# RWKV-6 attention with a GELU MLP behind it: each product, evacuation, sum, bank fill and block copy becomes a step of its own, in a new order

## The chip, the cores and the metric

One core of one Trainium2 chip runs the whole kernel. The metric is device time in microseconds, the median of several executions. Engines in the text: PE is TensorE, PEld its weight load, DVE is VectorE, ACT is ScalarE, POOL is GpSimd, SP is SyncE, which here issues most DMAs. Each engine works through its own list of instructions in the order in which the program wrote them, and waits on semaphores where an instruction needs another engine's result.

## The reference

The first half is a recurrence over 768 positions for 4 x 8 heads of width 48, the second an MLP on the 3072 tokens with 384 channels:

```python
for t in range(S):
    cur = einsum('bhd,bhe->bhde', u * k[t], v[t])
    y[t] = einsum('bhd,bhde->bhe', r[t], state + cur)
    state = w[t][..., None] * state + einsum('bhd,bhe->bhde', k[t], v[t])
x = y.transpose(0, 2, 1, 3).reshape(3072, 384)
h = x @ w_in                       # 384 -> 2048
out = (0.5 * h * (1 + erf(h / sqrt(2)))) @ w_out
```

All of it is float32.

## The kernel before

**Tiles and stages.** The 3072 tokens are eight tiles of 384 (half of one batch each). `attention(x, unit)` and `mlp(x)` are generators: each `yield` ends a step. The loop at the end of the kernel runs stage x: the attention of tile x beside the MLP of tile x-1, and the first steps of the attention of tile x+1. A string `PLAN[x]` says which generator makes its next step: "." the MLP of tile x-1 (in stage 0 the first half of the heads, unit 0), "s" what is left of the attention of tile x (in stage 0 unit 1), "f" the attention of tile x+1, "l" the loads on SP, "c" the conversion of the weights from 64-bit words, "w" sums of weights, "x" the five sums of the finished x, `sums_of_x`. The order in which steps are made is the order in every engine's list, so PLAN alone decides what queues behind what. After the loop the MLP of tile 7 runs alone.

**The attention of a tile from 2 on** (`quarters`). DVE makes sums of products of k and r for blocks of four positions (L427 to L470; the next tile's part starts with four multiplies, L441) and small totals of w (L462). `plain` (ACT, three copies, L610) and `lay_out` (DVE, two multiplies, L615, L616) lay out r. Then come three bursts of small matmuls (L641) for blocks of 4 and three for blocks of 16, each into a pair of PSUM banks, of which there are two pairs; `copy_quarters` empties a pair, for 4 with three masked copies on DVE (L674), for 16 with six copies on ACT (L657). k is transposed in four blocks on DVE (L589), and twelve blocks are moved by DMAs from SP (L584), four by ACT (L751). From these come the kv products (L768), the state chain on DVE (`chain_states`, L784, L789), the inside products (L810), a small "fence" copy on DVE (L822), the products with the state (L857), and the copies of y into xT (ACT L880, L883; six DMAs L887).

**The MLP of a tile from 1 on.** Both matrix products use fast schemes with fewer multiplications. Up (`h_halves`): for each of four groups q seven products, with the letters of the new code: A x00, E with t1, B completes the bank of A, F, G and D accumulate in a bank `u`, which is filled with a copy of A's result, and C completes the bank of E. ACT evacuates each: gelu, a copy into g, or a save that an accumulating DMA from POOL (L1029), for q = 3 an add on DVE (L1031), adds to g. A step is a product with its evacuation and what hangs on it. Down (`g_fast`): twenty products a to t of sums of g (`G_SUMS`, DVE, L1185) in the fixed order of `G_ORDER`; six chains of products share four banks (`G_BANKS`), two of which are filled with zeros first (L1162); results go to rows by ACT (L1173) or are added on DVE (L1175). A step here is the sums that a product needs, the product (L1190), its result, and the fill of the next bank. The last group's last products, D3 with its gelu and two more, are run behind product a. The two banks `mm` hold A and E in turn, then the chains of a and of b.

**Tile 0** uses plain products (`h_plain`, L1115, `g_plain`, L1126), in stage 1.

Of the kernel before, what the change touches and what calls it, by code (L numbers as in the profile page):

```python
# [10 lines left out]
F32 = mybir.dt.float32  # L11
# [29 lines left out]
        ".lls.....slscs.lsslll.sl.sls..sl.lscsl..sss.lscs.lscs.ss.clll.s..s.cccss...wss..ss.ff"  # L41
    ),
    1: (
        "c.scscc.cs.c.cs.ccscccs.w.lcscccss.ccccc.lwcs.scc..cc.c.ccsc.cc.lcccc.ccsc.cl.cc.sclccclws"
        ".scs..s.cscllcc.wcs.ccwlw.wcsccs.fww.s.f.f...f..wwfwfx.wf..fx.fxlfxffxw"
    ),
    2: (
        "www....wlwsw.ww..w..wws.....sss.wws.sws..ss.slss..ws.wss.w.s.sslssww.ws.s...lss..l.lss.lsl"
        "s.l..s.f...sf.f.f.x.xx.f.lxx"
    ),  # L50
    3: (
        "ss.l...ss.sl.s.s.....s...ss.ss.ssll.s..lsss.s.s.sss..sssssss.s...l.s....sl.sll...s.s.fsff."
        ".fs.fl...xxx.ffxfxf"
    ),
    4: (
        "ll........ss.....s.s...ssl..s.sl.sss...s.ssss...sss.s.s.l.ssssl.ss..s....ss.lss.l.slfs.f.f"
        ".f.xl.xxfxfffxff"
    ),
# [4 lines left out]
    6: (  # L63
        "s..s...s.s....ls.ss..s...ssls...ss..sss.ss.ss.....sss.s.s..sss.ls.....sss.ll.lslss.lslf..s"
        "f.fffs.lx.x.xffffxx"
    ),
    7: (
        ".......ss....s.s...s.ssssss...sss.ss...sss..ssss.s....s.s..s..s..s.s.s.s.ss..x.x...xxx"
# [26 lines left out]
W_ORDER = "empsiclratkdjfnbohqg"  # L95

# [6 lines left out]
def kernel(  # L103
# [298 lines left out]
    def attention(x, unit):  # L402
# [190 lines left out]
        def quarters():  # L593
# [13 lines left out]
            def plain(h):  # L607
                m, r4, t4, s0, s1, s2 = views(h)
                for z, f in ((s0[:, :, :, 0:h], 1), (s1[:, :, :, 0:h], 2), (s2, 3)):
                    nc.scalar.copy(out=z, in_=r4[:, :, :, f, :])  # L610

            def lay_out(h):
                m, r4, t4, s0, s1, s2 = views(h)
                z = s1[:, :, :, h:]
                nc.vector.tensor_mul(z, r4[:, :, :, 3, :], t4[:, :, :, 2:3].to_broadcast(z.shape))  # L615
                nc.vector.tensor_mul(s0[:, :, :, h:], s1, t4[:, :, :, 1:2].to_broadcast(s1.shape))  # L616

            plain(FINE)
            lay_out(FINE)
            yield  # L620
            n_b = np_ * NI
            for h in QUARTERS:
# [27 lines left out]
                def copy_rows(first, behind, d, g):  # L650

                    for p in range(2):
                        for a, rows in ((1, slice(0, 2 * h)), (0, slice(0, h)), (2, slice(2 * h, 3 * h))):
# [3 lines left out]
                            nc.scalar.copy(out=at[z, g, first:behind, (a + 1) * h:], in_=d[z, :, :, to] if g == slice(None) else d[z, :, to])  # L657

                def copy_quarters(first, behind, d):
                    if isinstance(d, list):  # L660
                        for g in range(2):
                            copy_rows(first, behind, d[g][:, 0:(behind - first) * 3 * C // 2].rearrange("p (n x) -> p n x", n=behind - first), g)
                        return
                    d = d[:, :, 0:(behind - first) * 3 * C // 2].rearrange("p g (n x) -> p g n x", n=behind - first)
                    if m == 1:
                        copy_rows(first, behind, d, slice(None))
                        return
                    an = at[:, :, first:behind].rearrange("p g n (m x) -> p g n m x", m=m)
                    o = 0
                    for a in range(3):  # L670
# [3 lines left out]
                        nc.vector.copy_predicated(out=an[:, :, :, :, (a + 1) * h:], mask=mask.to_broadcast(data.shape), data=data)  # L674
                        o += w_q
# [13 lines left out]
                copy_quarters(*parts_of[0], ds[0])  # L689
                yield  # L690
# [7 lines left out]
                if not last:  # L698
                    plain(4 * h)
# [9 lines left out]
                if not last:  # L709
                    lay_out(4 * h)  # L710
# [6 lines left out]
                for z, d in list(zip(parts_of, ds))[1:]:  # L717
                    copy_quarters(*z, d)
                    yield
# [253 lines left out]
    def sums_of_x(x):  # L973

        assert x in done and (x == 1 or (x - 1, "h") in behind)
# [7 lines left out]
    def mlp(x):  # L983


        xT = xT_of.pop(x)
        gs = {}

        def store(row0, o_sb, c0=0):
            nc.sync.dma_start(out=out[row0:row0 + 128, c0:c0 + o_sb.shape[1]], in_=o_sb)  # L990
# [4 lines left out]
        late = []  # L995

        def h_halves():

            x00, t1, x10, x11, l0, l1 = (xT[:, c, b * HT:(b + 1) * HT] for c in range(3) for b in range(2))
            t2, t3, t4, l01 = x_sums  # L1000

# [6 lines left out]
            def two(o, q, *factors, start=False):  # L1008
                for i in range(2):
# [12 lines left out]
            def saved(o):  # L1022
                z = wk.tile([128, DM], F32, name="o_sb", bufs=2)
                nc.scalar.copy(out=z, in_=o)  # L1024
                return of_two(z)

            def add_to(q, o, z):
# [5 lines left out]
            def first(q):  # L1033
                a_of[q] = h_bank()
                two(a_of[q], q, (w(0, 0), x00), start=True)
# [3 lines left out]
            def second(q):  # L1039
                two(a_of[q], q, (w(0, 1), x10), (w(0, 2), l0))  # L1040
                gelu(q, 0, 0, of_two(a_of[q]))

            def third(q):
                two(z_of[q], q, (s(4), x11), (w(0, 2), l1))
                add_to(q, g_of(q, 0, 1), saved(z_of[q]))

            def fourth(q):
                two(u_of[q], q, (w(1, 1), t4), (w(1, 2), l01))
                gelu(q, 1, 0, of_two(u_of[q]))

            def fifth(q):
                z_of[q] = h_bank()
                two(z_of[q], q, (s(1), t1), start=True)
                nc.scalar.copy(out=g_of(q, 1, 1), in_=of_two(z_of[q]))

            def sixth(q):
                two(u_of[q], q, (s(2), t2))
                nc.scalar.copy(out=g_of(q, 0, 1), in_=of_two(u_of[q]))

            def seventh(q):  # L1060
                two(u_of[q], q, (s(3), t3), (w(1, 2), l1))
                add_to(q, g_of(q, 1, 1), saved(u_of[q]))

            def h_bank():
                return bank("h_ps")[:, 0:2 * HT]

            a_of, z_of, u_of = {}, {}, {}
            for group in (0, 2, 1, 3):
                gs[group] = gp.tile([128, FG, T], F32, name="g")
            for q in range(HK):  # L1070
                assert q // 2 in ready
                first(q)
                if q > 1:
                    gelu(q - 2, 1, 1, g_of(q - 2, 1, 1))
                yield
                if q:
                    third(q - 1)
                    yield
                    seventh(q - 1)
                    yield  # L1080
                else:
                    fifth(q)
                    yield
                second(q)
                yield
                if q:
                    fifth(q)
                    yield
                sixth(q)
                yield  # L1090
                if q:
                    fourth(q - 1)
                    gelu(q - 1, 0, 1, g_of(q - 1, 0, 1))
                    yield
            q = HK - 1
            seventh(q)
# [225 lines left out]
```

## Time and profile before

| | us |
|---|---|
| median of 3 runs | 595.72 |
| the runs | 592.74, 596.96, 595.72 |
| the profiled execution | 595.25 |
| its span, first to last instruction | 593.4 |
| last stage, MLP of tile 7 alone | 59.0 |
| copies out of burst pairs on ACT, L657, 108 of them | 39.0 |
| state chain on DVE, L784, 160 of them | 29.3 |

A row of the profile names engine, line, operation, tile written and tiles read, shape, and count; "busy" is the time in which at least one instruction of the group ran, and the idle time in brackets is what the engine waited just before, with the instruction that ended the wait. The granted TensorE clock was 1.00 in every stage.

### The profile page before, as it was taken

What the parts mean: (1) busy time and instruction counts of PE and PEld (TensorE: products, weight loads), DVE (VectorE), ACT (ScalarE), POOL (GpSimd) and SP (SyncE); (2) the same over time, 40 slices, a digit from 0 to 9 for tenths busy, and PEclk for the clock granted to TensorE, in tenths of its full rate; (3) what the DMA queues carried; (4) which work ended last, traced back from release to release, by engine and by line L of the source; (5) the groups of instructions that cost most, each with busy time, mean ns of one, the idle gap of its engine ahead of it and who ended that gap; (6) DMA issues with size and microseconds to landing.
All of it is one profiled execution on the core that took longest, in us unless ns stands there. A gap on an engine that the chain in (4) does not pass through costs nothing.

```text
span 593.4 us, 17546 instructions
## 1 busy us (share of the span) xinstructions
PE 569.0 (96%) x7530; PEld 509.6 (86%) x7544; DVE 451.5 (76%) x880; ACT 290.1 (49%) x634; POOL 58.7 (10%) x63
## 2 busy tenths in 40 slices
PE   6789999999999999999999999999999999999997
PEld 3566656679899998999998989999999899999997
DVE  6878947999988987896786987897796987640171
ACT  2366989235642558035562356425544465525520
POOL 3100000002100130003100121003100021002200
PEclk9999999999999999999999999999999999999999
DMA  6668661134250642245213632425315342203401
GB/s 236 197 196 304 229 216 56 39 107 55 36 140 14 182 67 37 78 141 94 28 32 87 166 83 28 94 46 125 40 19 149 92 55 31 40 12 66 54 1 40
DMA packets 61854, 55.07 MB, mean 93 GB/s; under 512 B 32337, under 2 KB 46929, under 8 KB 61777
## 3 DMA queue, kind: packets, MB, share of 16 engines
q1 hardware_dynamic: 50256, 45.62, 25.6%
q0 software_dynamic: 11424, 8.26, 10.8%
q8 instruction: 59, 0.97, 0.7%
q14 instruction: 19, 0.15, 0.1%
q10 hardware_dynamic: 96, 0.07, 0.1%
HBM read 36.24 MB, written 4.72 MB: 69 GB/s over the span
## 4 chain that ended last, share of the span: by engine, by line
PE 84%; DVE 7%; ACT 4%; DMA 2%; issue 2%; SPq 1%; DVEq 0%
PE h_ps L993 17%; PE u_ps L1190 15%; PE u_ps L993 15%; PE o_ps L1190 11%; PE o_ps L1126 5%; PE h_ps L1115 5%; PE d L641 4%; PE d L504 3%; PE kv_ps L768 2%; PE y_ps L857 2%; PE y_ps L810 2%; DMA rkw<-in_rkw_dram 2%; ACT g L1020 2%; ACT a_sb L657 1%; DVE rkw L470 1%
## 5 line engine op out<-in xcount | busy, mean ns | idle before, releaser
L993 PE MATMUL h_ps<-xT,w_in_sb 128*128 128x192 f32 x560 | 111.7, 330 | 2.0 <-DVE xT L980 1.6
L1029 POOL DMA_DIRECT2D g<-o_sb x42 | 50.7, 1244 | 488.4 <-ACT o_sb L1024 486.6
L993 PEld LDWEIGHTS h_ps<-xT,w_in_sb 128*128 128x128 f32 x560 | 93.1, 190 | 6.2 <-DVE xT L980 2.2
L1190 PE MATMUL u_ps<-w_out_sb,g 128*128 128x192 f32 x224 | 41.5, 329 | 0.0
L993 PE MATMUL u_ps<-s,w_in_sb 128*128 128x192 f32 x224 | 41.2, 327 | 0.0
L657 ACT COPY a_sb<-d 32x320 f32<-32x320 f32 (+5 forms) x108 | 39.0, 361 | 3.4 <-PE d L641 1.6
L1190 PE MATMUL o_ps<-t,g 128*128 128x192 f32 x224 | 40.0, 327 | 0.6 <-ACT o_sb L1024 0.6
L1190 PEld LDWEIGHTS o_ps<-t,g 128*128 128x128 f32 x224 | 36.9, 190 | 0.9 <-ACT o_sb L1024 0.9
L993 PEld LDWEIGHTS u_ps<-s,w_in_sb 128*128 128x128 f32 x224 | 37.1, 190 | 0.2
L1190 PEld LDWEIGHTS u_ps<-w_out_sb,g 128*128 128x128 f32 x224 | 36.9, 190 | 0.3
L1173 ACT ACTIVATE o_sb<-u_ps 128x192 f32<-128x192 f32 x21 | 6.9, 330 | 53.9 <-PE u_ps L1190 53.7
L1126 PE MATMUL o_ps<-w_out_sb,g 128*128 128x384 f32 x96 | 33.0, 494 | 0.0
L1190 PE MATMUL u_ps<-w_extra,g 128*128 128x192 f32 x168 | 31.6, 331 | 1.5 <-ACT u_ps L1162 1.5
L641 PE MATMUL d<-kx,rkw 64*64 64x96 f32 x1152 | 30.0, 247 | 2.5 <-ACT a_sb L657 1.7
L1115 PE MATMUL h_ps<-xT,w_in_sb 128*128 128x384 f32 x96 | 32.3, 492 | 0.0
L641 PEld LDWEIGHTS d<-kx,rkw 64*64 64x64 f32 x1152 | 25.1, 133 | 7.5 <-ACT a_sb L657 3.3
L1190 PEld LDWEIGHTS u_ps<-w_extra,g 128*128 128x128 f32 x168 | 27.4, 190 | 3.3 <-ACT u_ps L1162 3.0
L674 DVE COPY_PREDICATED a_sb<-quarter,d 128x480 f32<-128x480 uint8 (+5 forms) x54 | 23.1, 438 | 9.1 <-PE d L641 7.9
L1031 DVE TENSOR_TENSOR g<-g,o_sb 128x384 f32<-128x384 f32 x14 | 7.7, 548 | 29.2 <-ACT o_sb L1024 29.1
L784 DVE SCALAR_TENSOR_TENSOR st<-st,tot_sb,kv_ps 128x48 f32<-128x48 f32 x160 | 29.3, 256 | 0.7 <-PE kv_ps L768 0.6
L504 PEld LDWEIGHTS d<-rkw 64*64 64x64 f32 x1152 | 19.1, 134 | 12.5 <-issue 7.0
L1020 ACT ACTIVATE g<-g 128x384 f32<-128x384 f32 x56 | 28.4, 520 | 1.1 <-DMA g<-o_sb 0.8
(163 smaller groups left out, 1195.6 us busy)
## 6 DMA issues: line engine op xcount, KB each, us to landing
rkw<-in_rkw_dram SPq DMA_DIRECT2D x54, 256.0 KB, 3.7
g<-o_sb POOLq DMA_DIRECT2D x42, 192.0 KB, 3.6
raw<-in_w_out_dram SPq DMA_DIRECT2D x8, 768.0 KB, 4.5
v_in<-in_v_dram SPq DMA_DIRECT2D x8, 584.0 KB, 4.6
raw<-in_w_in_dram SPq DMA_DIRECT2D x5, 768.0 KB, 6.8
rkw<-kx SPq DMA_DIRECT2D x72, 48.0 KB, 2.0
out_dram<-o_sb SPq DMA_DIRECT2D x17, 192.0 KB, 2.0
rkw<-in_rkw_dram SPq DMA_DIRECT2D x6, 384.0 KB, 5.2
```

Of the source, the lines that this page charges most:

```text
L504: nc.tensor.matmul(d[half[p], g, n * width:(n + 1) * width], lhsT=kc[half[g], b, i, p], rhs=right(half[g], b, i, p), start=True, stop=True)
L641: nc.tensor.matmul(o[half[p], i * 3 * C // 2:(i + 1) * 3 * C // 2], lhsT=kc[half[g], n // NI, n % NI, p], rhs=rx[half[g], 2 * n + p], star ...
L657: nc.scalar.copy(out=at[z, g, first:behind, (a + 1) * h:], in_=d[z, :, :, to] if g == slice(None) else d[z, :, to])
L674: nc.vector.copy_predicated(out=an[:, :, :, :, (a + 1) * h:], mask=mask.to_broadcast(data.shape), data=data)
L768: nc.tensor.matmul(kv_ps[half[g], p, i * D:(i + 1) * D], lhsT=k_t(b, i, p, g), rhs=vs(b, i, g)[half[p], 0:D], start=True, stop=True)
L784: nc.vector.scalar_tensor_tensor(out=stq[:, q, c], in0=stq[:, q, c - 1] if c else b4[:, q, NC - 1], scalar=totq[:, q, c:c + 1], in1=kvs[q ...
L993: nc.tensor.matmul(o, lhsT=lhsT, rhs=rhs, start=start, stop=True, skip_group_check=True)
L1020: nc.scalar.activation(out=g_of(q, a, b), in_=z, func=AF.Gelu)
L1029: nc.gpsimd.dma_start(out=o, in_=z, accum_op=ALU.add)
L1115: nc.tensor.matmul(h_ps, lhsT=w_in_sb[:, f // FI, j, f % FI * 128:(f % FI + 1) * 128], rhs=xT[:, j, :], start=(j == 0), stop=(j == NJ - 1))
L1126: nc.tensor.matmul(o, lhsT=gs[f // FG][:, f % FG, i * 128:(i + 1) * 128], rhs=w_out_sb[:, f, :], start=(f == 0), stop=(f == NF - 1))
L1190: nc.tensor.matmul(held[chain], lhsT=a(G_PRODUCTS[z])[:, j], rhs=w_place[z][:, j], skip_group_check=True, start=G_BANKS[chain][0] == "m" a ...
```

## The change

`PLAN` is replaced for all stages; a "." is now a single operation, so strings are longer. In the MLP of tiles 1 to 7 `h_halves`, `g_fast` and `G_ORDER` give way to two tables of operations and `ORDER[x]`, a list of 131 operations for each tile: the letters with a group number are those above (capitals products, small letters what follows them), "+" a sum, "=" a product, "!" its result to the rows, "<" the fill of a bank. `ORDER[7]` lists the operations in the order in which the code before makes them. In the attention each copy of a burst's pair, each copy of `plain`, each half of `lay_out` and each block copy of k on ACT gets its own `yield` (76 steps for a tile where there were 43). The rows of the output get their buffer when first written instead of at the start of the second product. No operation is added, removed or resized. Tables 2, 3, 5 and 6 and most of PLAN are left out of the diff below; this table counts from all of them how many large products (A to G, a to t) stand between two places of a stage, before and after the change:

| stage | ahead of the first burst | first to last burst of 16 | k transposes to kv | kv to inside | inside to state products | state products to the end | C3 to product b |
|---|---|---|---|---|---|---|---|
| 2 | 9, 5 | 3, 3 | 9, 14 | 4, 4 | 4, 3 | 6, 7 | 2, 4 |
| 3 | 15, 14 | 2, 2 | 10, 11 | 6, 3 | 2, 1 | 5, 6 | 2, 3 |
| 4 | 17, 18 | 1, 2 | 7, 10 | 3, 3 | 0, 0 | 5, 5 | 2, 4 |
| 5 | 15, 19 | 2, 2 | 8, 11 | 4, 2 | 1, 0 | 5, 5 | 2, 3 |
| 6 | 16, 18 | 1, 2 | 8, 10 | 3, 3 | 1, 1 | 3, 4 | 2, 4 |
| 7 | 15, 15 | 2, 2 | 12, 10 | 4, 3 | 0, 1 | 6, 6 | 2, 2 |

```diff
 PLAN = {
     0: (
-        ".lls.....slscs.lsslll.sl.sls..sl.lscsl..sss.lscs.lscs.ss.clll.s..s.cccss...wss..ss.ff"
+        "lllll.lll.lll.l.s.s.ssssss..sc.sssl.s.lcl.s.s.s.s..lcls.ssc.s.c.s.s.cs..cscss.s.sfwf."
     ),
...
     5: (
-        "l........ss....s.l..ss.sssl.s.l.ss.lsss...ssssl..sss.s...s.ss.s..s....ss.s.slll.f.sf.sff.f"
-        "x...xl.xxx"
+        "s..s.s.......s..s..s....s.......s..s........sss..s...sss....sl.ss.sss.sssss....s...ss.sss...s....s.."
+        "s.ls..sl.s.ss.s.s.s.s.s...s..s..s.s.s.sls.s.ssllsss.s.....sss.s..........s..s.........ss..s.llss..l."
+        ".ss.f...f.f..fxx.xxl.fx."
     ),
...
-G_ORDER = (
-    "a +22 +e5 b +e2 i +03 g +23 +e0 +e1 k +e3 +01 +E3 +E2 j +00 h +20 c +e4 m +E0 "
-    "+E4 q l n s p f o t r d e"
-)
 W_ORDER = "empsiclratkdjfnbohqg"
+ORDER = {
+    1: (
+        "A0 a0 E0 e0 F0 B0 C0 b0 f0 A1 G0 c0 a1 E1 g0 B1 e1 F1 k0 f1 D0 b1 G1 A2 l0 C1 g1 d0 a2 j0 B2 c1 l1 E2 F2 "
+        "e2 b2 i0 k1 A3 f2 j1 C2 D1 c2 d1 G2 a3 g2 E3 F3 D2 e3 d2 l2 f3 i1 B3 b3 C3 k2 G3 <i c3 g3 k3 l3 =a i2 i3 "
+        "D3 j2 +01 d3 <g j3 =i +00 !b =b +23 =g +03 !a =k +22 +e0 +e5 +e1 !g +e2 +e3 =j +E2 !j +E3 !k =h !h =c =m "
+        "!c +20 !m +e4 =q !q =l <p =n !n !i +E0 +E4 !l =s !s =o =p !p =f =t !f !o =r !t !r =d =e !e !d"
+    ),
...
+    4: (
+        "A0 E0 a0 e0 B0 F0 b0 C0 f0 A1 G0 c0 k0 a1 F1 g0 E1 B1 f1 D0 b1 e1 d0 G1 A2 C1 l0 a2 g1 B2 c1 F2 b2 E2 i0 "
+        "A3 e2 k1 D1 d1 C2 a3 l1 j1 f2 j0 G2 c2 k2 g2 F3 E3 e3 i1 f3 B3 D2 C3 c3 l2 d2 i2 G3 j2 +22 g3 b3 =a k3 "
+        "D3 l3 +e5 <i i3 +e2 d3 !a j3 +03 +23 =b +01 <g =g +e0 =k +e1 =i =j !g +e3 =c !k !j =h +E3 !d +E2 !h +00 "
+        "+20 =m !i =q !m !q +e4 =l +E4 !l =n +E0 =s !c !s <p !n =p =f !p !f =o =t !o !b !t =r !r =d =e !e"
+    ),
...
+    7: (
+        "A0 a0 E0 e0 B0 b0 F0 f0 A1 a1 C0 c0 k0 G0 g0 l0 B1 b1 E1 e1 F1 f1 D0 d0 i0 A2 a2 j0 C1 c1 k1 G1 g1 l1 B2 "
+        "b2 E2 e2 F2 f2 D1 d1 i1 A3 a3 j1 C2 c2 k2 G2 g2 l2 B3 b3 E3 e3 F3 f3 D2 d2 i2 G3 g3 l3 j2 C3 c3 k3 =a !a "
+        "D3 d3 i3 j3 +22 +e5 =b !b <i +e2 =i !i <g +03 =g !g +23 +e0 +e1 =k !k +e3 +01 +E3 +E2 =j !j +00 =h !h "
+        "+20 =c !c +e4 =m !m +E0 +E4 =q !q =l !l =n !n =s !s <p =p !p =f !f =o !o =t !t =r !r =d !d =e !e"
+    ),
+}
...
                     nc.scalar.copy(out=z, in_=r4[:, :, :, f, :])
+                    yield
 
             def lay_out(h):
                 m, r4, t4, s0, s1, s2 = views(h)
                 z = s1[:, :, :, h:]
                 nc.vector.tensor_mul(z, r4[:, :, :, 3, :], t4[:, :, :, 2:3].to_broadcast(z.shape))
+                yield
                 nc.vector.tensor_mul(s0[:, :, :, h:], s1, t4[:, :, :, 1:2].to_broadcast(s1.shape))
 
-            plain(FINE)
-            lay_out(FINE)
+            yield from plain(FINE)
+            yield from lay_out(FINE)
...
                             nc.scalar.copy(out=at[z, g, first:behind, (a + 1) * h:], in_=d[z, :, :, to] if g == slice(None) else d[z, :, to])
+                            yield
...
                 assert (x - 1, "at") in behind
-                copy_quarters(*parts_of[0], ds[0])
-                yield
+                yield from copy_quarters(*parts_of[0], ds[0])
...
                 nc.scalar.copy(out=block_of_kt(z, z), in_=kb[z * 32:(z + 1) * 32, z])
+                yield
...
+            def begin(of, q, o, *factors):
+                of[q] = o[:, 0:2 * HT]
+                two(of[q], q, *factors, start=True)
+
+            def fill(q):
                 u_of[q] = bank_u(q)[:, 0:2 * HT]
                 nc.scalar.copy(out=u_of[q], in_=a_of[q])
 
+            return {
+                "A": lambda q: begin(a_of, q, bank("h_ps"), (w(0, 0), x00)),
+                "a": fill,
+                "B": lambda q: two(a_of[q], q, (w(0, 1), x10), (w(0, 2), l0)),
+                "b": lambda q: gelu(q, 0, 0, of_two(a_of[q])),
+                "C": lambda q: two(z_of[q], q, (s(4), x11), (w(0, 2), l1)),
+                "c": lambda q: save(q, 0, z_of[q]),
+                "k": lambda q: add(q, 0, 1),
+                "D": lambda q: two(u_of[q], q, (w(1, 1), t4), (w(1, 2), l01)),
+                "d": lambda q: gelu(q, 1, 0, of_two(u_of[q])),
+                "E": lambda q: begin(z_of, q, bank("h_ps"), (s(1), t1)),
+                "e": lambda q: nc.scalar.copy(out=g_of(q, 1, 1), in_=of_two(z_of[q])),
+                "F": lambda q: two(u_of[q], q, (s(2), t2)),
+                "f": lambda q: nc.scalar.copy(out=g_of(q, 0, 1), in_=of_two(u_of[q])),
+                "G": lambda q: two(u_of[q], q, (s(3), t3), (w(1, 2), l1)),
+                "g": lambda q: save(q, 1, u_of[q]),
+                "l": lambda q: add(q, 1, 1),
+                "i": lambda q: gelu(q, 0, 1, g_of(q, 0, 1)),
+                "j": lambda q: gelu(q, 1, 1, g_of(q, 1, 1)),
+            }
...
+            def product(p):
+                chain = chain_of[p]
+                if chain not in held:
+                    assert G_BANKS[chain][0] == "m"
+                    open_bank(p)
+                for j in range(FG):
+                    multiply(held[chain], a(G_PRODUCTS[p])[:, j], w_place[p][:, j], G_BANKS[chain][0] == "m" and p == chain[0] and j == 0)
...
-            for z in tokens:
-                if z[0] == "+":
-                    x_, op, y_ = G_SUMS[z[1:]].split()
-                    (nc.vector.tensor_add if op == "+" else nc.vector.tensor_sub)(*(a(i) for i in (z[1:] if z != "+E0" else "20", x_, y_)))
-                    continue
...
-        row0 = x * T
-        if x:
-            yield from h_halves()
-            yield from g_fast()
-        else:
+            return {"+": add, "<": open_bank, "=": product, "!": end}
+
+        if not x:
             yield from h_plain()
             yield from g_plain()
+            return
+        ops = {**h_ops(), **g_ops()}
+        order = ORDER[x].split()
+        assert len(set(order)) == len(order) == 18 * HK + len(G_SUMS) + 2 * len(G_PRODUCTS) + sum(z[0] == "u" for z in G_BANKS.values())
+        for z in order:
+            ops[z[0]](int(z[1:]) if z[1:].isdigit() and z[0] not in "+<=!" else z[1:])
+            behind.add((x, z))
+            yield
```

More of the change, by code (lines that the diff above doesn't have):

```diff
@@ L1060, in seventh @@
[L1060 to L1080, printed above, removed]
-                else:
[L1082 to L1094, printed above, removed]
@@ L1169, in end @@
                     i, n = int(z[2]), int(z[3])
+                    if i not in rows:
+                        rows[i] = wk.tile([128, DM], F32, name="o_sb", bufs=2)
                     to = rows[i][:, n * HM:(n + 1) * HM]
```

155 lines of the change are left out of this document (60 added, 95 removed), and 20 rows, old and new, of the table ORDER.

## The prediction

> **What bounds the kernel now.** I read the page from the top, then the busy time of each stage, then who waits on TensorE, then the places in order of time. Stage x is the attention of tile x beside the MLP of tile x-1; the cuts are the starts of each tile's first product A0.
>
> ```profile
> span 593.4 us, 17546 instructions
> PE 569.0 (96%) x7530; PEld 509.6 (86%) x7544; DVE 451.5 (76%) x880; ACT 290.1 (49%) x634; POOL 58.7 (10%) x63
> ```
>
> Second view, the stages. Columns: stretch, its length, busy us of PE, weight load, DVE, ACT, POOL, granted clock, DMA share, GB/s.
>
> ```profile
> 0.00:45.00 45.00, 33.22 (x1082) 23.65 (x1096) 34.42 (x106) 19.70 (x33) 7.98 (x21) 1.00 0.65 209
> 45.00:125.60 80.60, 80.59 (x1073) 50.78 (x1074) 64.83 (x106) 53.92 (x77) 0.00 (x0) 1.00 0.46 155
> 125.60:194.00 68.40, 66.90 (x833) 63.25 (x834) 63.32 (x121) 33.10 (x81) 7.37 (x6) 1.00 0.37 82
> 194.00:261.70 67.70, 66.79 (x851) 63.49 (x850) 56.86 (x106) 32.75 (x80) 7.23 (x6) 1.00 0.37 79
> 261.70:329.60 67.90, 66.29 (x832) 63.48 (x832) 53.17 (x101) 32.78 (x80) 7.23 (x6) 1.00 0.35 80
> 329.60:398.20 68.60, 66.76 (x851) 63.63 (x850) 59.12 (x111) 32.74 (x80) 7.23 (x6) 1.00 0.36 81
> 398.20:467.80 69.60, 67.22 (x838) 63.83 (x836) 56.38 (x108) 33.47 (x81) 7.20 (x6) 1.00 0.37 81
> 467.80:534.40 66.60, 66.05 (x846) 63.27 (x847) 46.95 (x93) 32.37 (x79) 7.28 (x6) 1.00 0.27 48
> ```
>
> TensorE bounds it from 45 us on. Stage 1 idles 0.01 us. In stages 2 to 7 length minus busy PE gives 1.50, 0.91, 1.61, 1.84, 2.38 and 0.55: 8.8 us. No other engine fills a stage; DVE comes nearest (63.32 of 68.40). The operations stay, so a new order can win little beyond those 8.8 us and what stage 0 holds.
>
> Third view: who ended TensorE's waits in stages 2 to 7 (us in total, times, longest).
>
> ```profile
> PE d L641 <- ACT a_sb L657: 1.7, 3, 0.6
> PE h_ps L993 <- DVE xT L980: 1.6, 2, 1.0
> PE u_ps L1190 <- ACT u_ps L1162: 1.2, 4, 0.3
> PE o_ps L1190 <- ACT o_sb L1024: 1.1, 2, 0.6
> PE d L641 <- DVE kx L616: 0.8, 1, 0.8
> PE y_ps L857 <- DVE fence L822: 0.8, 3, 0.4
> PE kv_ps L768 <- DMA rkw<-kx: 0.4, 1, 0.4
> PE y_ps L810 <- DVE st L784: 0.4, 1, 0.4
> PE h_ps L993 <- DMA xT<-ysb: 0.4, 1, 0.4
> ```
>
> Eighteen waits, 8.4 us. A wait costs a little more than its row says:
>
> ```profile
> 306.09 1.46 PE L1190 MATMUL u_ps<-w_extra,g 128*128 128x192 f32 x8
> 307.39 1.46 PE L1190 MATMUL o_ps<-w_out_sb,e 128*128 128x192 f32 x8
> ```
>
> One product lasts 1.46 us, yet the next starts 1.30 after it. Idle time counts from the modelled end, so a stall loses its row plus 0.16. That makes 1.30 the price of an eight-matmul step (B, C, D, G, "="), and 0.65 that of A, E and F.
>
> **The change part by part.** It adds and removes no operation; counts of matmuls, evacuations and DMAs are the same, and so are the runs of small matmuls between large ones (41 in the tables of stages 2 to 7 before, 40 after). Only waits change.
>
> *Waits that the coarse steps made.* Three places:
>
> ```profile
> 296.36 2.58 ACT L657 COPY a_sb<-d 32x320 f32<-32x320 f32 x6
> 298.99 0.56 PE L641 MATMUL d<-kx,rkw 64*64 64x96 f32 x16 [0.57 <-ACT a_sb L657]
> 230.98 1.57 PE L1190 MATMUL o_ps<-w_out_sb,g 128*128 128x192 f32 x8 [0.57 <-ACT o_sb L1024]
> 232.76 1.57 PE L1190 MATMUL u_ps<-w_extra,g 128*128 128x192 f32 x8 [0.21 <-ACT u_ps L1162]
> ```
>
> The last burst of the 16-step needs the bank pair that six copies (2.58 us) empty. In stages 2, 4 and 6, where the wait is, 2.6, 1.3 and 1.3 us of large products stood between the first burst and the last; the new tables put 3.25, 2.6 and 2.6 there. Product b takes the bank of C3 two products later, while its evacuation c3 queues on ACT; the new tables for stages 2 to 6 leave three or four. The fill "<i" was issued behind d3, i3 and j3; now it stands ahead of d3 in stages 2 to 6 (stage 7 keeps it behind, but i is the sixth product there instead of the third). So 1.7 + 1.2 + 1.1 = 4.0 us and nine restarts of 0.16: -5.4. If an evacuation ahead of the fill is late, as much as the old rows comes back, no more than 0.73 a place.
>
> *First burst and kv.* The wait on kx (0.8, stage 5) goes: 18.2 us of products now precede that burst in its stage, 14.95 before: -1.0. kv waits on the block moves:
>
> ```profile
> 310.93 0.62 SPq L584
> 311.60 2.03 DMA rkw<-kx
> 313.76 1.57 PE L768 MATMUL kv_ps<-v_in,rkw 64*64 64x48 f32 x90 [0.40 <-DMA rkw<-kx]
> ```
>
> In stage 4 seven products lay between transposes and kv, now ten: 3.9 us more against 0.4: -0.6. Elsewhere 10 to 14 lie there (8 to 12 before). On SP at most one load (stage 3) stands among the twelve moves, 0.6 us by the move's row, within that cover. Stage 2 moves the first burst from nine products into the stage to five; nearest row is the 0.8 wait of the same burst: 0 to 0.8, I take +0.6: six of DVE's weight-sum steps still stand ahead of it (eleven before).
>
> *Into the end of a tile.* From kv to the inside products:
>
> ```profile
> 452.30 1.57 PE L1190 MATMUL u_ps<-w_out_sb,g 128*128 128x192 f32 x8
> 456.40 1.63 PE L810 MATMUL y_ps<-a_sb,v_in 64*64 64x64 f32 x96
> 452.58 2.18 DVE L784 SCALAR_TENSOR_TENSOR st<-st,tot_sb,kv_ps 128x48 f32<-128x48 f32 x12
> 454.94 1.48 DVE L784 SCALAR_TENSOR_TENSOR st<-st,tot_sb,kv_ps 128x48 f32<-128x48 f32 x8
> 456.34 3.06 DVE L441 SCALAR_TENSOR_TENSOR kx<-rkw,u_sb 128x384 f32<-128x384 f32 x4
> 459.97 1.45 PE L857 MATMUL y_ps<-rkw,st 64*64 64x64 f32 x80 [0.45 <-DVE fence L822]
> ```
>
> The y pairs reuse kv's banks, so the state chain must end first: kv ends at 452.3, the chain at 456.4, 4.1 us; three products (3.9) just cover it. Before, the six stages had 4, 6, 3, 4, 3, 4 products there; now 4, 3, 3, 2, 3, 3. Stage 5 has 2.6 us against 3.9 to 4.1: +1.4. Stages 3 and 7 lose their cover while row adds still stand inside the chain: +0.45 each. The fence waits (0.8) stay: stage 7 loses one, stage 5 gets one, and stage 6 still puts the next tile's four multiplies (3.06) on DVE ahead of the fence. Behind these DVE instructions wait the sums of x and so A0's successors: in stage 4 one block of small totals leaves the queue ahead of the sums and the 0.57 at the start of stage 5 goes: -0.7. In stage 6 four products follow the last y matmuls instead of three, which covers the xT DMA (0.4); the sums still come late: -0.4.
>
> Stages 2 to 7: -5.4 -1.0 -0.6 +0.6 +1.4 +0.9 -0.7 -0.4 = **-5.2 us**. The last MLP runs table 7, which is today's order step for step: 0.
>
> *Stages 0 and 1.* Stage 1 stays full of TensorE. In stage 0, twelve of the seventeen load steps now come before the first unit's update of r (two of them before). DVE has 34.42 us of work in 45 and cannot start until data lands, so I take 0, between -2 and +3. What may be lost:
>
> ```profile
> PEld d L504 <- issue: 6.5, 7, 1.4
> PE d L504 <- issue: 2.5, 3, 1.3
> ```
>
> These are waits of the matmul queue in the first 46 us that no semaphore explains, at a DMA share of 0.65; none of over a microsecond appears after. The Trainium skill, Runtime: NRT & Kernel Launch, "Instruction fetch mechanics", says that instruction fetch is hidden by the sequencer's own pace; by it fuller queues would cost nothing. The trace does not fit that well, but names no cause.
>
> The profiled execution took 595.25 us, 1.85 outside its span, and the median of the runs shown is 595.72. 595.25 - 5.2 = **590.0 us**.
>
> **The rivals.** *Slower: blocked queues* (0.24). The block copies and burst copies, six to twelve in a row before, now stand singly between evacuations that each wait for a product in an in-order queue.
>
> ```profile
> ACT o_sb L1173 <- PE u_ps L1190: 43.9, 14, 6.6
> ```
>
> ACT waits up to 6.6 us for such an evacuation today. If each of the last copies ahead of kv comes one product late, then kv, the state chain and the next x come late by 1.3 to 2.6 us a stage: 8 to 16 us over six stages, 590 + 8 to 16 = 598 to 606. It decides from 0.9 us a stage, where it eats the 5.2. For it: in stage 6 the last block copy now stands directly ahead of kv. Against: ACT is busy 33 of 68 us.
>
> *Slow start* (0.10): the issue waits (6.5 us at the weight loads; those of the matmuls lie within them) grow by a half through the earlier loads: +3, 593; if they double, 596.5.
>
> *All waits go* (0.15): 8.4 us, 18 restarts (2.9), and up to 2 in stage 0: 595.25 - 11 to 13 = 582 to 584; half of it 587.
>
> *It moves nothing* (0.04): one wait replaces another, 595.
>
> *More room than the idle time shows* (0.03). Weight loads fill 63.49 of 67.70 us in stage 3, so 4.2 us a stage would be free, 25 over six: 570. Against it, uninterrupted products already follow each other at 1.30 us, which no order changes. The Trainium skill, Perfetto Trace Analysis, "Identifying the Most-Contended Engine", asks to judge TensorE's headroom by weight-load share instead of matmul busy time; by that rule it would be this case.
>
> **How the numbers follow.** The forecast's case has 0.44: 586 to 594. About 1% can be told from no change, so faster means under 589.8 and slower over 601.7. Faster: half of the forecast's case (0.22), all waits gone (0.15), more room (0.03): 0.40. Slower: a good half of the blocked queues, 0.13, and 0.01 of the slow start: 0.14. Within: 0.46. The range 583 to 601 leaves out the 570 case, the lower end of "all go" and the upper half of the blocked queues, under 0.2.
>
> **What would show it.** Right: in the waits of TensorE the rows from L657, L1162 and L1024 shrink to at most the last tile's one, kv no longer waits on a DMA, and y_ps L810 on st grows to about 2 us. Wrong: kv_ps or d rows that name ACT at over 2 us, stages 2 to 7 of over 68 us, or a first product of the MLP later than 46 us.

## The result, and the profile after

The changed kernel took 587.31 us (median of 4 runs, 586.66 to 588.03), the kernel before beside it 594.78 (4 runs): a ratio of 0.9874, with a 95% interval of 0.9834 to 0.9914. The profiled execution took 587.29 us. It is faster by 1.3%, and the forecast of 590.0 was 2.7 us too high.

The page of the changed kernel begins so. All lines have moved by 46 to 52 (L641 is now L689, L657 L705, L810 L859, L857 L906); both matrix products of the MLP now stand on L1043.

```profile
span 585.5 us, 17564 instructions
PE 566.6 (97%) x7544; PEld 510.5 (87%) x7544; DVE 451.5 (77%) x880; ACT 290.7 (50%) x634; POOL 58.9 (10%) x63
```

The stages, with the same columns as before and cut again at each A0; the rows are those of stages 0 to 2, 5, 7 and the last MLP:

```profile
0.00:49.11 49.11, 37.65 (x1194) 26.46 (x1195) 37.17 (x113) 21.78 (x37) 7.98 (x21) 0.97 0.56 187
49.11:127.34 78.23, 78.06 (x974) 49.31 (x975) 66.29 (x106) 51.74 (x73) 0.00 (x0) 1.00 0.49 170
127.34:193.26 65.92, 65.92 (x834) 63.19 (x833) 60.27 (x113) 32.91 (x81) 7.37 (x6) 1.00 0.34 71
...
324.95:392.93 67.98, 66.16 (x850) 63.69 (x849) 56.77 (x107) 32.74 (x80) 7.27 (x6) 1.00 0.37 83
...
459.07:526.03 66.96, 65.98 (x849) 63.44 (x849) 48.14 (x96) 32.48 (x80) 7.24 (x6) 1.00 0.26 48
526.03:585.50 59.47, 55.49 (x338) 54.38 (x336) 16.91 (x37) 19.35 (x45) 7.20 (x6) 1.00 0.21 40
```

By the matmuls' rows stage 2 now has no idle time. The same cuts taken exactly in both traces give the balance: stages 2 to 7 take 398.69 us where they took 408.58 (-9.89), stage 2 begins at 127.34 where it began at 125.64 (+1.70), and the last MLP takes 59.47 where it took 59.18 (+0.29). Together -7.9, the difference of the spans. So the order won more than forecast in the middle and lost something at the start.

Who ends TensorE's waits in stages 2 to 7 after the change:

```profile
PE y_ps L906 <- issue: 1.3, 1, 1.3
PE h_ps L1043 <- DVE xT L1029: 1.3, 2, 1.0
PE y_ps L906 <- DVE fence L871: 0.3, 2, 0.2
PE y_ps L859 <- DVE st L833: 0.3, 1, 0.3
```

Six waits, 3.2 us, where there were eighteen, 8.4 us. The rows of the burst copies, of the zero fill, of the save of C3, of kx and of the block moves are gone. One row is new: a wait on issue of 1.3 us.

The rows fell by 5.2 us and the stages by 9.9. That 5.2 is also the forecast's figure is a coincidence: the forecast's held 0.16 for each restart, and by that price twelve waits fewer make 7.1. The rest shows at the weight loads, whose waits the forecast did not go through. Busy time of each engine over stages 2 to 7 as one stretch, first before, then after:

```profile
125.64:534.22 408.58, 399.83 (x5040) 380.76 (x5040) 335.74 (x637) 197.16 (x481) 43.54 (x36) 1.00 0.35 75
```

```profile
127.34:526.03 398.69, 395.41 (x5041) 380.34 (x5040) 331.16 (x627) 197.87 (x481) 43.67 (x36) 1.00 0.35 76
```

The same 5040 weight loads take the same time (380.76 and 380.34), but the same matmuls are "busy" 4.4 us less. A matmul's row runs to a modelled end, and whatever small delay lies before the next one disappears under it. The weight load does not cover it: stretch less weight-load busy is 27.8 us before and 18.35 after, a difference of 9.5. The waits of the weight loads in these stages, before (the longest rows):

```profile
PEld d L641 <- ACT a_sb L657: 3.3, 6, 0.9
PEld u_ps L1190 <- ACT u_ps L1162: 2.4, 4, 0.6
PEld d L641 <- issue: 2.2, 10, 0.2
PEld h_ps L993 <- DVE xT L980: 2.2, 2, 1.3
PEld o_ps L1190 <- ACT o_sb L1024: 1.7, 2, 0.9
PEld y_ps L857 <- DVE fence L822: 1.4, 3, 0.7
PEld h_ps L993 <- ACT g L1020: 1.3, 6, 0.2
PEld kv_ps L768 <- issue: 1.3, 6, 0.2
PEld d L641 <- ACT o_sb L1024: 1.1, 1, 1.1
...
PEld h_ps L993 <- ACT u_ps L1037: 0.8, 4, 0.2
```

and the longest after:

```profile
PEld d L689 <- issue: 2.7, 12, 0.2
PEld y_ps L906 <- issue: 2.1, 4, 1.5
PEld h_ps L1043 <- DVE xT L1029: 1.9, 2, 1.3
PEld kv_ps L817 <- issue: 1.3, 6, 0.2
```

All rows of this view add up to 23.6 us before and 14.4 after: -9.2. Those that name an engine or a DMA fall from 17.5 to 6.1, those on issue (no semaphore explains them) grow from 6.1 to 8.3. The same copies (L657) that cost TensorE 1.7 us in three waits by the matmuls' rows cost 3.3 in six by the weight loads'; the gelus of L1020 and the bank fills of L1037, 2.1 us in ten waits of at most 0.2, have no row among the matmuls at all. The Trainium skill, Perfetto Trace Analysis, "Identifying the Most-Contended Engine", asks to judge TensorE by the weight loads instead of matmul busy time; here the traces agree.

### The profile page after: what moved, and what is told of

It reads as the page before. It is cut to its first block, busy times and chain, and to the rows that moved or that the text cites. A ratio compares the mean times of both kernels' runs of the same rounds, so it can differ in the third digit from the quotient of the medians.

```text
span 585.5 us, 17564 instructions
## 1 busy us (share of the span) xinstructions
PE 566.6 (97%) x7544; PEld 510.5 (87%) x7544; DVE 451.5 (77%) x880; ACT 290.7 (50%) x634; POOL 58.9 (10%) x63
## 4 chain that ended last, share of the span: by engine, by line
PE 90%; DVE 3%; issue 2%; DMA 2%; ACT 1%; SPq 1%; ACTq 0%; DVEq 0%
PE u_ps L1043 31%; PE h_ps L1043 19%; PE o_ps L1043 13%; PE h_ps L1121 5%; PE o_ps L1133 5%; PE d L689 5%; PE d L550 3%; PE y_ps L859 2%; PE y_ps L906 2%; PE kv_ps L817 2%; DMA xT<-ysb 1%; PE warm L324 1%; SPq L936 1%; DMA rkw<-in_rkw_dram 1%; DVE tot_sb L508 1%
## 5 line engine op out<-in xcount | busy, mean ns | idle before, releaser
L1043 PE MATMUL h_ps<-xT,w_in_sb 128*128 128x192 f32 x560 | 110.1, 329 | 1.4 <-DVE xT L1029 1.3
L1043 PEld LDWEIGHTS h_ps<-xT,w_in_sb 128*128 128x128 f32 x560 | 93.2, 190 | 4.2 <-DVE xT L1029 1.9
L705 ACT COPY a_sb<-d 32x320 f32<-32x320 f32 (+5 forms) x108 | 39.1, 362 | 6.6 <-PE d L689 4.9
L1043 PE MATMUL u_ps<-s,w_in_sb 128*128 128x192 f32 x224 | 41.4, 328 | 0.0
L1043 PE MATMUL u_ps<-w_out_sb,g 128*128 128x192 f32 x224 | 41.3, 328 | 0.0
L1043 PE MATMUL o_ps<-t,g 128*128 128x192 f32 x224 | 40.6, 327 | 0.0
L1043 PEld LDWEIGHTS o_ps<-t,g 128*128 128x128 f32 x224 | 36.9, 190 | 0.5 <-ACT o_sb L1076 0.3
L1043 PEld LDWEIGHTS u_ps<-s,w_in_sb 128*128 128x128 f32 x224 | 36.9, 190 | 0.5
L1043 PEld LDWEIGHTS u_ps<-w_out_sb,g 128*128 128x128 f32 x224 | 36.9, 190 | 0.3
L723 DVE COPY_PREDICATED a_sb<-quarter,d 128x480 f32<-128x480 uint8 (+5 forms) x54 | 23.1, 438 | 12.9 <-PE d L689 11.7
L1091 ACT COPY u_ps<-h_ps 128x384 f32<-128x384 f32 x28 | 13.1, 467 | 36.5 <-PE h_ps L1043 36.1
L1043 PE MATMUL u_ps<-w_extra,g 128*128 128x192 f32 x168 | 30.7, 327 | 0.3 <-ACT u_ps L1167 0.3
L932 ACT COPY ysb<-y_ps 128x384 f32<-128x384 f32 x8 | 3.8, 480 | 53.7 <-PE y_ps L906 42.9
L689 PE MATMUL d<-kx,rkw 64*64 64x96 f32 x1152 | 29.4, 247 | 0.0
```

The lines of the kernel that those rows point to most:

```text
L689: nc.tensor.matmul(o[half[p], i * 3 * C // 2:(i + 1) * 3 * C // 2], lhsT=kc[half[g], n // NI, n % NI, p], rhs=rx[half[g], 2 * n + p], star ...
L1043: nc.tensor.matmul(o, lhsT=lhsT, rhs=rhs, start=start, stop=True, skip_group_check=True)
L1091: nc.scalar.copy(out=u_of[q], in_=a_of[q])
```

## The experiments

Each kernel ran beside the kernel before on one chip; ratios are to that, with 95% intervals.

**The changed kernel again.** No edit.

> The changed kernel as it is, on the same chip as the other two: 587.3 within 1. It also tells how much the start scatters from run to run: if the MLP starts again at 49.1 us and stage 2 at 127.3, the loss in stage 0 is of the order; if it starts up to a microsecond earlier, that much of it is scatter.

588.20 us, ratio 0.9885 (0.9865 to 0.9904). Stages 2 to 4, 6 and 7 took the same to 0.02 us, stage 5 took 0.3 less and the last MLP 0.4 more, so the +0.29 above is within the scatter. The start differed: the MLP began at 50.34 us and stage 2 at 128.20. So the start scatters, and here it was later still. In the six traced kernels with the new start stage 2 begins at 125.89 to 128.52 (mean 127.1), in the four with the changed tables and the old start below at 123.94 to 126.59 (mean 125.2), in the three with the old tables and the old start at 125.48 to 125.99 (mean 125.7). Much of this goes with the granted clock: in the first 50 us the two latest of the new start (128.52 and 128.20) show 0.50 for 10.2 and 13.7 us, the other four for 3.4 us each; of the four with the changed tables and the old start only the latest shows it, for 3.4 us.

**The start.** Two kernels, one with the old string of stage 0, one with the new order but late loads:

```diff
-        "lllll.lll.lll.l.s.s.ssssss..sc.sssl.s.lcl.s.s.s.s..lcls.ssc.s.c.s.s.cs..cscss.s.sfwf."
+        ".lls.....slscs.lsslll.sl.sls..sl.lscsl..sss.lscs.lscs.ss.clll.s..s.cccss...wss..ss.ff"
```

```diff
+        ".ll...s.s.lssslssllls.l.slc.sssl.ls.lc.s.s.sl.s.l.cs.ssc.llls.c.s.s.cs..cscss.s.sfwf."
```

> The changed kernel with the old PLAN string for stage 0 alone. Theory (the new order of stage 0 runs the small matmuls of both units closer together, and TensorE waits for its own instructions): the 2.9 us wait of y_ps L859 on issue goes, the first product of the MLP starts at about 45.8 instead of 49.1 us, stage 2 starts 1.7 us earlier (one step of 96 small matmuls lies in stage 1 again), the time falls from 587.3 to about 585.6. Rival (stage 0 makes no difference to the end, since stage 1 waits for something else): 587.3 and stage 2 still starts at 127.3.

> The changed kernel with its new order of the two units in stage 0, but the 17 load steps as far back as in the old string. Theory (issue waits come from the order of the small matmuls): the wait of about 2.9 us on issue stays, the MLP starts at 49 us or later, 587.3 or more. Rival (the early loads hold up the fetch of instructions and of the first data): the MLP starts at about 46 us and the time falls by 1.7 us to 585.6.

The old start gave 584.81 us, ratio 0.982 (0.980 to 0.984): the 2.9 us wait is gone and stage 2 begins at 125.59, 1.75 earlier. Late loads gave 585.91, ratio 0.9835 (0.982 to 0.9849); stage 2 begins at 126.40, but the wait stays at 2.5 us and the MLP begins at 48.54. So the long wait goes with the order of the small matmuls. The time came out near the rival's 585.6 all the same; the 0.9 us that stage 2 begins earlier is within the scatter, so what the early loads cost stays open. TensorE in the start of the changed kernel, timeline:

```profile
35.55 0.78 PE L859 MATMUL y_ps<-a_sb,v_in 64*64 64x64 f32 x39
39.27 1.40 PE L859 MATMUL y_ps<-a_sb,v_in 64*64 64x64 f32 x57 [2.94 <-issue]
40.43 2.05 PE L906 MATMUL y_ps<-rkw,st 64*64 64x64 f32 x34
```

The new string runs kv of both units, then the inside products of both, then those with the state, with no transposes between. In the middle of one run of 96 equal matmuls TensorE stands still for 2.94 us. A packet of the instruction queue begins at 36.98, 2.3 us before TensorE resumes; hardly anything else moves on the DMA engines then, as the DMA share (the last column but one) in these windows of 2 us shows:

```profile
38.00:40.00 2.00, 0.73 (x41) 0.73 (x44) 0.31 (x2) 0.03 (x1) 0.00 (x0) 0.95 0.00 0
40.00:42.00 2.00, 2.00 (x57) 2.00 (x52) 1.97 (x13) 0.00 (x0) 0.00 (x0) 0.50 0.03 8
42.00:44.00 2.00, 2.00 (x103) 2.00 (x100) 0.66 (x3) 0.48 (x1) 0.00 (x0) 0.70 0.03 8
44.00:46.00 2.00, 2.00 (x67) 1.68 (x61) 1.93 (x3) 0.00 (x0) 0.00 (x0) 1.00 0.11 25
```

The column before it is the granted clock: after the standstill it is 0.50 and 0.70, and 34 matmuls last 2.05 us; with late loads the same 34 last 1.17 us, at a clock of 1.00. With the old start all five windows from 36 to 46 us show 1.00. The Trainium skill, TensorE: Matmul & The Clock Gate, "What's actually happening", says that an idle window of about 3.4 us halves the clock and a busy one restores it. The trace agrees in kind and in the length of the slow stretch (0.50 from 39.78 to 43.19 us), but the standstill before it, 2.94 us, was shorter than that window.

**The old MLP order.** The last table for all tiles, first with the new PLAN as it is, then with the attention's steps moved so that each stands behind as many large products as in the changed kernel; and the reverse, the new tables with the attention behind as many products as before the change (the moved strings are left out):

```diff
+ORDER = {x: ORDER[7] for x in ORDER}
```

> The changed kernel with the old order of the MLP's operations (the last table) for every tile; PLAN and the attention in small steps stay. Theory (the new order of products and evacuations removed the waits): rows of TensorE from L1024's counterpart (the save of C3) and from the zero fill return in stages 2 to 7, 3 to 6 us with their restarts, time 590 to 594. Rival (the attention in small steps brought the gain): no such rows over 1 us in sum, 587.3 within 1.

> The changed kernel with the old order of the MLP's operations for every tile, and with PLAN rewritten so that each step of the attention stands behind the same number of large products as in the changed kernel. Theory (the new order of products and evacuations removed the waits): the waits for the save of C3 ahead of product b and for the zero fill ahead of i come back in stages 2 to 7, 3 to 5 us with their restarts, time 590 to 592. Rival (where the attention's steps stand brought the gain, the MLP's own order nothing): those rows under 1 us in sum, 587 to 588.

> The changed kernel with its new order of the MLP's operations and its small steps, but in stages 2 to 7 the steps of the attention, loads and sums stand behind the same number of large products as before the change. Theory (the two tables fit each other, and neither order brings the gain alone; the old MLP order with new places took 630 to 640): evacuations and copies meet in ACT's and DVE's queues, waits of the weight loads in stages 2 to 7 grow from 14 to over 25 us, time over 598. Rival (the new MLP order is better wherever the attention stands): 590 or less, weight-load waits at most 17 us.

629.64, 638.61 and 642.12 us, ratios 1.0571 (1.0544 to 1.0598), 1.072 (1.0683 to 1.0758) and 1.0806 (1.0786 to 1.0827). Both sides of the first two expectations fell, and the theory of the third held: neither the new MLP order nor the new places hold the gain, for either alone costs 42 to 55 us. The weight-load waits of stages 2 to 7 grow to 53.8, 59.5 and 60.7 us. Waits of TensorE in the second of the three (the longest rows):

```profile
PE d L691 <- ACT a_sb L707: 9.8, 6, 2.8
PE u_ps L1045 <- ACT u_ps L1169: 8.7, 7, 3.8
PE h_ps L1045 <- DVE xT L1031: 5.1, 4, 2.7
```

One of them, on ACT and TensorE (stage 3):

```profile
235.42 0.49 ACT L1074 ACTIVATE g<-u_ps 128x384 f32<-128x384 f32 x1 [2.78 <-PE u_ps L1045]
235.81 1.27 ACT L707 COPY a_sb<-d 32x320 f32<-32x320 f32 x3
237.10 0.52 ACT L1074 ACTIVATE g<-g 128x384 f32<-128x384 f32 x1
237.65 0.48 ACT L1078 COPY o_sb<-u_ps 128x384 f32<-128x384 f32 x1
238.15 1.29 ACT L707 COPY a_sb<-d 32x320 f32<-32x320 f32 x3
239.50 0.56 PE L691 MATMUL d<-kx,rkw 64*64 64x96 f32 x16 [2.82 <-ACT a_sb L707]
```

The copies that free the burst's pair have a gelu ahead of them that waits 2.78 us for its product, and a gelu and a save among them; the burst waits for all of it. In the old kernel the six stood together, and the longest such wait was 0.6.

**Grouped copies.** The new order, but each group of copies (those of r and of k too) at the place of its first member:

```diff
+def together(steps):
+    n = sum(1 for _ in steps)
+    for _ in range(n):
+        yield
...
-                yield from copy_quarters(*parts_of[0], ds[0])
+                yield from together(copy_quarters(*parts_of[0], ds[0]))
```

> The changed kernel with the copies of each burst's pair, the three copies of plain r, the two multiplies that lay it out and the four block copies on ACT made together again, each group where its first member stands in the new order. Theory (the MLP's order brought the gain): 587.3 within 1, with at most 1 us of new waits. Rival (small steps in the attention brought it): waits on L657's counterpart and on evacuations that queue behind six copies return, 2 to 5 us, time 589 to 592.

588.94 us, ratio 0.9893 (0.9869 to 0.9917); stages 2 to 7 take 401.39 us, 2.7 more than in the changed kernel, 1.66 of it in stage 2. There the copy of A that fills the bank u stands behind the six burst copies, and the product waits:

```profile
151.32 2.58 ACT L711 COPY a_sb<-d 32x320 f32<-32x320 f32 x6
154.42 0.92 PE L1052 MATMUL u_ps<-s 128*128 128x192 f32 x4 [0.89 <-ACT u_ps L1100]
```

Without the small steps 2.7 of the 9.9 us are lost, between the two expectations.

**One term alone, in the kernel before.** The fill of i's bank issued behind product a; then with it b behind i, and in stages 2, 4 and 6 the last burst one product later:

```diff
                 end(z, chain)
+                if z == "a":
+                    begin("i")
```

```diff
-    "a +22 +e5 b +e2 i +03 g +23
+    "a +22 +e5 +e2 i b +03 g +23
```

> The kernel before with one edit: the zero fill of product i's bank is issued right behind product a, ahead of the last gelus of the up half. Theory: the five waits on L1162's counterpart, 1.5 us and five restarts of 0.16, go, and the time falls by 2.3 us, 594.8 to 592.5. Rival (b or i then waits for something else that is as late): the row goes, another of the same size takes its place, 594.8 within 0.5.

> The kernel before with the edit of the fill, product b behind i, and in stages 2, 4 and 6 the last burst of the 16-step one large product later. Theory (the first term of the forecast, alone): the rows from L657, L1162 and L1024 go, 5.4 us, 594.8 to 589.4. Rival (the terms do not add; what is removed here comes back at the next wait): above 592.5.

The fill alone: 592.00 us, ratio 0.9945 (0.9927 to 0.9964), the span 2.4 us shorter, as expected; the row is gone and nothing took its place. All three: 595.23 us, ratio 0.9997 (0.9982 to 1.0012), no gain. The waits show where it went:

```profile
PE kv_ps L767 <- DMA rkw<-kx: 2.5, 5, 1.1
...
PE u_ps L1189 <- ACT u_ps L1161: 0.8, 1, 0.8
...
PE o_ps L1189 <- ACT o_sb L1023: 0.6, 1, 0.6
```

kv waits for its block moves five times, 2.5 us where it was 0.4. Four of the five, 2.3 us, lie in stages 2, 4 and 6, where the burst was moved; that the later burst makes the moves later is the likely reason. One wait for a fill (0.8) and one for the save (0.6) are left as well. In the old kernel 7 to 12 products lie between the transposes and kv. In the changed kernel 10 to 14 products lie there.

**Stages 5 and 6 of the changed kernel.** Two attempts moved several steps at once. Both have the old start and, in the last tile, the zero fill ahead of D3. In stage 5 the first put the inside products one product earlier, so that a product lies between them and the state products; in the kernel that ran, kv and the state chain stayed where they were, since one of the steps moved is empty.

```diff
-        ".ss.f...f.f..fxx.xxl.fx."
+        "s.ls..sl.s.ss.s.s.s.s.s...s..s..s.s.s.sls.s.ssllsss.s.....sss.s..........s..s.....ss..s.....llss.sl."
+        "s...f...f.f..xxf.xxl.fx."
...
-        "..s.f...f..ff.xxf.xf.lfffffxx"
+        "..s.f...f...xxfff.xf.lfffffxx"
```

(The lines shown are those of the second attempt.)

> The changed kernel with the old PLAN string for stage 0; in stage 5 kv two products earlier, the inside products one earlier, and one large product between inside and state products; in stage 6 the state products one product earlier, the next tile's four multiplies behind them, and the first two sums of x ahead of the next tile's totals; in the last tile the zero fill ahead of D3. Theory (each remaining wait comes from its neighbours in the order): start -1.7, stage 5 -1.6 (the issue wait of 1.3 and the 0.3 on st go, since TensorE has a large product to run while instructions come in), start of stage 7 -1.1, last tile -0.4: 587.3 to 582.5. Rival (an issue wait falls at a fixed instruction number and stays, the sums of x wait for the xT transfers and stay): only the start gives, 585.6.

> The changed kernel with the old PLAN string for stage 0; in stage 5 kv two products earlier, inside and state products one and one earlier with a large product between them, no load moved behind the xT transfers; in stage 6 the first two sums of x ahead of the next tile's totals; in the last tile the zero fill ahead of D3. Theory (each remaining wait comes from its neighbours in the order): start -1.0, stage 5 -2.0 (issue wait of 1.3 and the waits on st and fence go), start of stage 7 -0.7, last tile -0.4: 4.1 less than the changed kernel beside it, about 583. Rival (issue waits stay at their instruction numbers, the sums of x wait for the xT transfers): only start and last tile give, 586.

594.98 us, ratio 0.9993 (0.9979 to 1.0007), and 590.48, ratio 0.9933 (0.9918 to 0.9947): both slower than the changed kernel, and neither expectation held. In the first, one load of the next tile's r, k and w now stands behind the state products, and so on SP behind the xT transfers:

```profile
393.28 1.58 DVE L487 SCALAR_TENSOR_TENSOR kx<-rkw,u_sb,rkw 128x384 f32<-128x384 f32 x2 [6.71 <-DMA rkw<-in_rkw_dram]
395.10 2.93 PE L1043 MATMUL u_ps<-w_out_sb,g 128*128 128x192 f32 x8 [5.01 <-DVE o_sb L1190]
```

DVE waits 6.71 us for that load, a row's add behind it on DVE waits with it, and so does the product that reuses the add's bank. That product then lasts 2.93 us where others last 1.46: the granted clock is 0.50 from 394.67 to 398.08. Stage 5 takes 74.58 us. In the second, kv waits up to 1.7 us for its block moves in stage 5, and in stage 6 the sums of x stand ahead of the next tile's totals:

```profile
459.14 0.36 DVE L1029 TENSOR_TENSOR s<-xT 128x192 f32<-128x192 f32 x1 [1.67 <-DMA xT<-ysb]
465.81 0.43 PE L1043 MATMUL u_ps<-s 128*128 128x192 f32 x1 [2.33 <-DVE s L1029]
```

The first sum waits for the xT transfer, DVE stands idle for 1.67 us, and the work that filled that time now delays the third sum and product F0 by 2.33: stage 7 takes 70.17 us where it took 66.96. The longer wait (2.33 for 0.98) makes 1.35 of this 3.2; behind it the granted clock is 0.50 from 467.22 to 470.63 us, which by estimate (half of 3.41) loses about 1.7. So the 1.0 us at the start of stage 7 hangs on the transfer and on DVE's queue at once, and putting the sums first does not remove it.

**One product moved.** Old start, the fill ahead of D3 in the last tile, and in stage 5 product o between the inside and the state products:

```diff
-        ".ss.f...f.f..fxx.xxl.fx."
+        ".s.sf...f.f..fxx.xxl.fx."
...
-        "D3 d3 i3 j3 +22 +e5 =b !b <i +e2
+        "<i D3 d3 i3 j3 +22 +e5 =b !b +e2
```

> The changed kernel with the old PLAN string for stage 0; in the last tile the zero fill ahead of D3; in stage 5 product o between inside and state products instead of behind them, nothing else moved. Theory (instructions come in while the large product runs, and only neighbours matter): start -1.4 (mean of the runs so far), last tile -0.6, stage 5 from 67.7 to about 66.8: 2.9 less than the changed kernel, about 585. Rival (with one product fewer behind the state products the xT transfers land late and the first products of stage 6 wait for them): stage 5 stays at 67.7 or more, 586 or more.

582.72 us, ratio 0.9799 (0.9772 to 0.9826): faster than both kernels. Stage 5 takes 66.29 us instead of 67.98, the last tile 58.7 instead of 59.47, and stage 2 begins at 123.94, the earliest of all. The span is 5.8 us shorter than in the changed kernel, and 3.4 of that lie ahead of stage 2, where the expectation had 1.4; the four kernels with this start scatter by as much as that (123.94 to 126.59). The state products now run without a gap:

```profile
377.91 1.63 PE L859 MATMUL y_ps<-a_sb,v_in 64*64 64x64 f32 x96 [0.33 <-DVE st L833]
379.47 1.57 PE L1043 MATMUL u_ps<-w_out_sb,g 128*128 128x192 f32 x8
380.96 1.63 PE L906 MATMUL y_ps<-rkw,st 64*64 64x64 f32 x96
```

In the changed kernel, where nothing stood between them, the same 96 matmuls came in three pieces, the last behind 1.32 us of waiting for instructions.

## Why the prediction was right, and where it was off

**The coarse steps' waits (-5.4).** Right that all three rows go in stages 2 to 7; only the last tile keeps its fill of 0.3, as forecast (by the matmuls' rows; at the weight loads 0.3 is left of the save's row). The price was too small: it took the matmuls' rows plus 0.16 a restart, while by the weight loads these three are 3.3 + 2.4 + 1.7 = 7.4. Taken out one by one the fill gave what it should (2.4 us of span), but all three in the old kernel gave nothing: kv's wait grew by 2.1, and 1.4 of the fill's and the save's stayed. The forecast counted the products before kv, 10 to 14 in the new tables, and so had a likely reason why they keep the gain.

**"The operations stay, so a new order can win little beyond those 8.8 us".** This bound is the step that failed: 9.9 were won. It left out the forecast's own restarts (8.8 and eighteen times 0.16 make 11.7) and took its measure from the matmuls' rows: idle TensorE by the matmuls was 8.8, by the weight loads 27.8. The rival "more room" had the right measure and the wrong amount: it gave all that room away, and 9.5 of it was taken.

**kx (-1.0), kv on the block moves (-0.6).** Both rows went.

**Stage 2's earlier first burst (+0.6).** It did not come; stage 2 has no wait.

**kv to inside (+1.4 in stage 5, +0.9 in stages 3 and 7).** Too large: 0.33 in stage 5, nothing in the others. The forecast let the chain begin when kv ends. In the trace it does not:

```profile
377.55 0.44 DVE L833 SCALAR_TENSOR_TENSOR st<-st,tot_sb,kv_ps 128x48 f32<-128x48 f32 x2 [0.52 <-PE kv_ps L817]
378.28 3.24 DVE L833 SCALAR_TENSOR_TENSOR st<-st,tot_sb,kv_ps 128x48 f32<-128x48 f32 x18 [0.29 <-PE kv_ps L817]
```

The next product follows kv at 378.11; two of twenty steps are done before that, and the chain ends 3.4 us behind it, not 4.1. So y_ps L859 waits 0.3 where the text asked for about 2. The fence waits, 0.8 that were to stay, are down to 0.3; the one of stage 6 went although the four multiplies still stand ahead of it.

**Sums of x (-0.7, -0.4).** The wait on the xT transfer and the 0.57 are gone, and the 1.0 at the start of stage 7 is still there (0.98). A new 0.30 stands at the start of stage 6.

**Not foreseen:** 1.3 us on issue in stage 5, from the three runs of 96 small matmuls that now stand close together.

**Start (0, between -2 and +3).** Measured +1.70 in the profiled pair, about +1.4 in the means against the old kernel's start and +1.9 against the changed tables with the old start: the sign that the text named as wrong, a first product later than 46 us (49.11), came true. The mechanism was that of the rival "slow start", waits on issue, at 1.7 us instead of its 3. Its cause does not fit: the long wait stays when the loads are late and goes with the old order of small matmuls. A halved clock came on top.

**Blocked queues.** This rival did not come about in the changed kernel, but the mechanism is real: three kernels with one table of each kind paid 42 to 55 us, and one load behind the xT transfers made TensorE wait for 5.0 and then run a product at half the clock. The sum of the errors: 4.7 too little gain in stages 2 to 7, 1.7 and 0.3 too little loss in stages 0 and 1 and the last MLP, which leaves the 2.7 us. That errors of both signs partly cancelled is luck.

What stays open: which of the hundreds of places in the two tables matter to the 9.9 us; only the fill (2.4, in the old kernel) and the splitting of the copies (2.7, in the new one) were priced alone, and these need not add.

## What to carry to other kernels

Read the room on TensorE from the weight loads' waits as well as the matmuls': a large product's row hid the first 0.16 us of a delay, and a shorter one altogether, and here what it hid was nearly half of the gain. An interleaving of two streams is one object: take over an order of one stream only together with the places of the other, and when a step is moved, follow every queue that it passes, loads on SP included. Between long runs of small matmuls leave a large product; here one such product took a wait of 1.3 us away.

## What the hardware showed unexpectedly

TensorE can outrun its own instruction fetch. Counted in the trace over matmuls, weight loads and the semaphore instructions of TensorE's queue, the waits on issue of 0.9 us and more among the matmuls' rows of the changed kernel come before instructions 705, 1217, 1729 and 10945, all multiples of 512 apart; they last 0.9 to 2.9 us, and each ends 2.3 to 2.8 us after the next packet of the instruction queue began. That queue moves 59 packets in the whole run, for 15242 such instructions about 258 each:

```profile
q8 instruction: 59, 0.97, 0.7%
```

From stage 2 on the changed kernel shows it in one place, in stage 5, where two runs of 96 small matmuls (192 instructions in 1.5 us each) stand side by side; in stage 4, where a run of 96 and one of 80 do, it doesn't. With a large product of 1.30 us and 16 instructions between the two, in the last experiment, the wait was gone.

A standstill can cost twice. Behind 2.94 us (the changed kernel's start), 2.40 (grouped copies, at the same place) and 2.33 (stage 7 of the second attempt) the granted clock was 0.50 for 3.41 us; behind 2.46 us (late loads) it stayed at 1.00. So the length of the standstill alone does not decide it.
